# Attention block with adaLN and MLP: last query block in two halves, shift passes of 2048 columns into buffers of their own, zero matmuls inside PV, due points for side work

## The chip, the cores and the metric

The kernel runs on one core of a Trainium2 chip. The metric is the device time of one execution in microseconds; lower is better. Each kernel was run several times, and medians with the lowest and highest are quoted. Runs called slow (over 1.5% above the fastest of the same kernel) are left out of comparisons. The granted TensorE clock is quoted as a share of full speed. "Half clock" is the time at 0.50. In the trace of before a PV set (explained below) started 0.216 us after another at 1.00 and 0.426 us after another at 0.50 (medians of direct successors).

Engines: PE is TensorE, PEld its weight loads, DVE is VectorE, ACT is ScalarE, POOL is GpSimd, SP issues transfers.

## The reference

One sequence of 2048 tokens, 512 features, 32 heads of 16, an MLP of 1376. Modulation vectors come from a condition `c`.

```python
sa, ca, ga, sb, cb, gb = split(silu(c) @ w_mod, 6)
h = layernorm(x) * (1 + ca) + sa
q, k, v = heads(h @ wqkv)
o = softmax(q @ k.T * 16**-0.5) @ v
x = x + ga * (o @ wo)
h = layernorm(x) * (1 + cb) + sb
x = x + gb * (gelu(h @ w1 + b1) @ w2 + b2)
```

## The kernel before

Attention is cut into 32 runs: four blocks of 512 queries, and in each block eight runs of four heads. A run goes over 16 key tiles of 128 keys. A key tile gives two score pairs ("halves"), each 128x1024 in PSUM, the memory that TensorE writes its results to. PV is the product of the exponentials with V; the four matmuls that do it for one key tile are a PV set. ScalarE takes the exponential of most of them. For three key tiles of each run (none in run 0) VectorE takes over with integer arithmetic: one pass writes the bit pattern of a rough exponential, five "shift passes" write shifted copies, and six PV sets with six scaled copies of V add up to a good one. So a run has 26 exponentials on ScalarE and 31 PV sets on TensorE.

The program has no dynamic order. A small scheduler inside the kernel (a Plan) holds every operation with an assumed duration, walks through time, and emits instructions in the order that it finds; a wrong assumption is an order that fits the chip badly. A Plan operation takes a buffer (`acq`) and gives it back when the operations that name it in `rel` are done.

The score buffers and the buffers of the VectorE key tiles:

```python
r_st = res("st", 3, [P, 2 * QB], FP32, pp)       # score pairs, PSUM, for ScalarE and VectorE alike
r_pt = res("pt", NPT, [P, 2 * QB], BF16)         # exponentials of ScalarE, NPT = 9
r_ph = Res("ph", 2, lambda i: [work.tile([P, 2 * QB], I16, name=f"ph{i}_{j}")
                               for j in range(NPH)])          # a set of six for one half, two sets

def exp_d(qk, r, kt, half):                      # VectorE's key tile, one half
    def go(o):
        n_d[1] += 1
        nc.vector.tensor_scalar(out=o.tile[0], in0=qk.tile, scalar1=PH_B, scalar2=0.0,
                                op0=ALU.add, op1=ALU.max)
    e = op("DVE", go, 1.25, (qk,), lat=0.05, prio=0.5, acq=r_ph, rel=(qk,))
    sh = [e]
    for j in range(1, NPH):
        sh.append(op("DVE", lambda o, j=j: nc.vector.tensor_scalar(
            out=e.tile[j], in0=e.tile[0], scalar1=PH_SH[j], scalar2=None, op0=ALU.add),
            0.335, (e,), lat=0.1, prio=2.0))
    o_e[(r, kt, half)] = (e, sh)
    if half == 1:
        lo, shl = o_e.pop((r, kt, 0))
        # ... cut
        for j in range(NPH):
            pv_op(r, kt, j, (shl[j], sh[j]),
                  lambda j=j: [lo.tile[j].bitcast(BF16), e.tile[j].bitcast(BF16)], (lo, e))
```

The last argument of `pv_op` names what the PV set gives back. All six sets name both halves' sets of six buffers, so the buffers of a key tile come free after the last of its six PV sets, and with two sets only one key tile can be in work.

Keeping the TensorE clock up: the scheduler adds up the TensorE work of its last 3.4 us and, where it falls under `HEAT`, puts a matmul on zeros into a gap of TensorE, if the gap is long enough:

```python
for t, us in reversed(self.done):
    tot += us
    if tot >= HEAT and not self.cool:            # HEAT = 1.6 us
        self.cool = t + WIN                      # WIN = 3.4 us
```

The last query block: after the last run everything that follows attention (Wo, second norm, MLP) is done for all four token tiles of 128 at the end (`last_block`), while the same work of the other blocks (`block_tail`) is side work hidden in the attention of the next block.

The softmax here doesn't subtract the row's maximum and nothing guards it: scores larger than these inputs give would overflow.

## Time and profile before

Measured 962.17 us (median of 4 runs, 958.86 to 965.45). The profiled execution is not one of these four: it took 973 us, with a span of 971.3 us.

| stretch of the profiled execution | us |
|---|---|
| head, to the first exponential on ScalarE | 21.5 |
| run 0 | 48.6 |
| runs 1 to 31 | 857.9 |
| tail, after the last exponential | 43.3 |

The page of the kernel before: span, busy time of the engines, and the clock in 40 slices (tenths of full speed).

```profile
span 971.3 us, 18012 instructions
...
PE 845.8 (87%) x7140; PEld 287.1 (30%) x7140; DVE 739.6 (76%) x1499; ACT 834.7 (86%) x888; POOL 86.5 (9%) x189
...
PEclk9897999876579999999979999987999999999989
```

The windows view of the kernel before, for run 0, runs 1 to 31 in one stretch, and the tail. Columns: stretch, its length, busy time and number of instructions of PE, PEld, DVE, ACT and POOL, granted clock, share of DMA, GB/s.

```profile
21.50:70.10 48.60, 38.72 (x338) 19.44 (x338) 26.62 (x62) 35.84 (x42) 16.04 (x42) 0.93 0.10 33
70.10:928.00 857.90, 757.03 (x6521) 243.02 (x6521) 681.50 (x1368) 781.99 (x816) 59.98 (x67) 0.93 0.08 21
928.00:971.30 43.30, 31.48 (x186) 18.06 (x185) 21.73 (x42) 13.25 (x28) 3.19 (x8) 0.92 0.04 13
```

ScalarE is the spine: 838 exponentials start 0.904 us apart where nothing holds them up. In runs 1 to 31 it is busy 782 of 858 us; summing its idle times of that stretch gives 74.4 us, nearly all of it waiting for score matmuls. TensorE is not idle meanwhile. Taking from the trace what it executed just before the awaited scores, for the length of each of the 132 gaps, it was busy with PV of VectorE's key tiles (about 29 us), side work (about 26 us) and other PV (about 18 us) that stood before the awaited scores in its order. (No view gives these sums, and they move by some 3 us with how overlapping matmuls are counted.)

The chain of waits of the kernel before, from the tail: Wo of four tiles, transposes, and the last W2 tiles, one after the other.

```profile
928.47 3.13 PE st_13383 L787 x14
931.60 3.02 PE st_13384 L787 x14
...
941.58 0.94 PE st_13453 L905 x7
...
961.70 2.48 PE st_13653 L795 x11
...
964.49 2.50 PE ax_13671 L795 x11
```

### The profile page before, as it was taken

What the parts mean: (1) busy time and instruction counts of PE and PEld (TensorE: products, weight loads), DVE (VectorE), ACT (ScalarE), POOL (GpSimd) and SP (SyncE); (2) the same over time, 40 slices, a digit from 0 to 9 for tenths busy, and PEclk for the clock granted to TensorE, in tenths of its full rate; (3) what the DMA queues carried; (4) which work ended last, traced back from release to release, by engine and by line L of the source; (5) the groups of instructions that cost most, each with busy time, mean ns of one, the idle gap of its engine ahead of it and who ended that gap; (6) DMA issues with size and microseconds to landing.
All of it is one profiled execution on the core that took longest, in us unless ns stands there. A gap on an engine that the chain in (4) does not pass through costs nothing.

```text
span 971.3 us, 18012 instructions
## 1 busy us (share of the span) xinstructions
PE 845.8 (87%) x7140; PEld 287.1 (30%) x7140; DVE 739.6 (76%) x1499; ACT 834.7 (86%) x888; POOL 86.5 (9%) x189
## 2 busy tenths in 40 slices
PE   8788888889988988888998898889988889888868
PEld 3432333222222322222322232222332233222234
DVE  5738798766577988858877888857787989858862
ACT  2687998988689988998989989997999999999934
POOL 3331111000000100000000101000000001000010
PEclk9897999876579999999979999987999999999989
DMA  5105001001100000000100000000100000000100
GB/s 174 66 1 129 13 13 35 13 10 48 34 13 13 13 2 19 7 17 23 41 12 14 13 3 20 5 11 18 46 18 12 14 3 13 13 17 19 46 1 22
DMA packets 31038, 24.41 MB, mean 25 GB/s; under 512 B 13709, under 2 KB 26350, under 8 KB 30954
## 3 DMA queue, kind: packets, MB, share of 16 engines
q1 hardware_dynamic: 30426, 23.26, 8.4%
q8 instruction: 56, 0.92, 0.4%
q14 instruction: 28, 0.23, 0.1%
q10 hardware_dynamic: 528, 0.00, 0.0%
HBM read 20.64 MB, written 2.61 MB: 24 GB/s over the span
## 4 chain that ended last, share of the span: by engine, by line
PE 43%; ACT 38%; DVE 10%; issue 8%; POOL 0%; ACTq 0%; DVEq 0%; POOLq 0%
PE od_3149 L670 1%; PE od_3522 L670 1%; PE od_7084 L670 1%; PE od_2773 L670 1%; PE od_3903 L670 1%; PE od_5144 L670 1%; DVE ln_s L433 1%; PE od_1023 L670 1%; PE od_1461 L670 1%; PE od_9472 L670 1%; PE od_10639 L670 1%; PE od_7464 L670 1%; ACT g_11410 L831 1%; ACT g_8235 L831 1%; PE od_1921 L670 0%
## 5 line engine op out<-in xcount | busy, mean ns | idle before, releaser
L670 PEld LDWEIGHTS <-VEB_92 128*32 128x32 bf16 x512 | 13.6, 94 | 30.4 <-issue 29.1
L670 PEld LDWEIGHTS <-VEB_91 128*32 128x32 bf16 x512 | 14.9, 98 | 21.5 <-issue 18.3
L670 PEld LDWEIGHTS <-VEB_90 128*32 128x32 bf16 x512 | 13.2, 95 | 25.9 <-issue 24.1
L670 PEld LDWEIGHTS <-VEB_89 128*32 128x32 bf16 x512 | 12.5, 99 | 27.2 <-issue 25.5
L606 PEld LDWEIGHTS <-kT_2_114 32*128 32x128 bf16 x128 | 8.3, 91 | 26.3 <-issue 24.8
L824 PEld LDWEIGHTS <-W_83 128*128 128x128 bf16 x132 | 10.5, 99 | 16.6 <-issue 9.3
L606 PEld LDWEIGHTS <-kT_2_118 32*128 32x128 bf16 x128 | 7.4, 91 | 26.2 <-issue 25.7
L606 PEld LDWEIGHTS <-kT_2_122 32*128 32x128 bf16 x128 | 7.1, 93 | 26.3 <-issue 26.1
L606 PEld LDWEIGHTS <-kT_3_119 32*128 32x128 bf16 x128 | 7.8, 91 | 23.8 <-issue 23.3
L606 PEld LDWEIGHTS <-kT_2_110 32*128 32x128 bf16 x128 | 7.3, 91 | 25.3 <-issue 24.6
L606 PEld LDWEIGHTS <-kT_1_109 32*128 32x128 bf16 x128 | 6.9, 93 | 25.6 <-issue 23.0
L606 PEld LDWEIGHTS <-kT_3_111 32*128 32x128 bf16 x128 | 6.9, 91 | 24.5 <-issue 23.1
L606 PEld LDWEIGHTS <-kT_0_108 32*128 32x128 bf16 x128 | 7.2, 91 | 23.3 <-issue 21.9
L606 PEld LDWEIGHTS <-kT_1_117 32*128 32x128 bf16 x128 | 7.0, 92 | 23.2 <-issue 22.6
L606 PEld LDWEIGHTS <-kT_1_121 32*128 32x128 bf16 x128 | 6.6, 92 | 24.3 <-issue 24.1
L606 PEld LDWEIGHTS <-kT_0_120 32*128 32x128 bf16 x128 | 6.9, 93 | 22.7 <-issue 22.6
L449 ACT ACTIVATE blk_13381<-st_13453,modB 128x256 bf16<-128x256 bf16 x2 | 1.0, 560 | 14.5 <-PE st_13453 L905 14.5
L606 PEld LDWEIGHTS <-kT_0_112 32*128 32x128 bf16 x128 | 6.7, 91 | 22.6 <-issue 21.7
L606 PEld LDWEIGHTS <-kT_0_116 32*128 32x128 bf16 x128 | 6.9, 91 | 20.9 <-issue 19.8
L606 PEld LDWEIGHTS <-kT_3_123 32*128 32x128 bf16 x128 | 6.9, 93 | 20.9 <-issue 20.4
L606 PEld LDWEIGHTS <-kT_1_113 32*128 32x128 bf16 x128 | 6.9, 91 | 20.6 <-issue 20.1
L606 PEld LDWEIGHTS <-kT_3_115 32*128 32x128 bf16 x128 | 6.9, 91 | 20.0 <-issue 18.4
(5858 smaller groups left out, 3496.4 us busy)
## 6 DMA issues: line engine op xcount, KB each, us to landing
W_83<-in_B_w_dram SPq DMA_DIRECT2D x1, 1376.0 KB
g_998<-in_w_mod_dram SPq DMA_DIRECT2D x2, 512.0 KB
xb_127<-in_A_x_dram SPq DMA_DIRECT2D x1, 512.0 KB
blk_135<-in_w_mod_dram SPq DMA_DIRECT2D x1, 512.0 KB
blk_145<-in_w_mod_dram SPq DMA_DIRECT2D x1, 512.0 KB
w_171<-in_A_wqkv_dram SPq DMA_DIRECT2D x1, 512.0 KB
w_176<-in_A_wqkv_dram SPq DMA_DIRECT2D x1, 512.0 KB
xb_180<-in_A_x_dram SPq DMA_DIRECT2D x1, 512.0 KB
```

Of the source, the lines that this page charges most:

```text
L433: nc.vector.bn_stats(out=st6, in_=src)
L449: nc.scalar.activation(out=dst, in_=src, func=ACT.Identity, bias=mod[:, j:j + 1], scale=mod[:, NC + j:NC + j + 1])
L606: nc.tensor.matmul(out=o.tile[:, g * QB:(g + 1) * QB], lhsT=kT[cc][kb][rows, ko * P:(ko + 1) * P], rhs=qm.tile[par][rows, :], start=True, ...
L670: nc.tensor.matmul(out=o_od[r].tile[32 * i:32 * i + 32, :], lhsT=v_tile(kt, ph)[:, c0:c0 + 32], rhs=got[i // 2][:, (i % 2) * QB:(i % 2 + 1 ...
L824: nc.tensor.matmul(out=o.tile, lhsT=W1[:, j, f * P:(f + 1) * P], rhs=h.tile[:, j, :], start=(j == 0), stop=(j == NC - 1))
L831: ge = op("ACT", lambda o: nc.scalar.activation(out=g.tile, in_=g.tile, func=ACT.Gelu_apprx_tanh), 4.9 + 2.6, ev, lat=-1.2, prio=0.5)
```

## The change

The intent, as far as the diff shows it: take half of the tail into attention; keep the clock up with zero matmuls in the tile positions of PV; fewer and longer passes on VectorE; an earlier start; side work spread by due points (a due point is the number of exponentials done from which the scheduler prefers a piece of side work); and longer latencies assumed in the plan, meant to be nearer to the chip.

```diff
-HEAT = 1.6
+HEAT = 1.3
+PEL = 0.24   # assumed latency after a matmul, was 0.2 or 0.25
+DL = 0.14    # after a shift pass, was 0.1
+DPL = 0.08   # after VectorE's first pass, was 0.05
+AL = 0.17    # after an exponential, was 0.15

+        if o.kind == "pv" and s >= self.cool and o.last_left() > 1:
+            o.extra, o.us = True, 2 * o.us
...
+            if o.extra:
+                for i in range(4):
+                    nc.tensor.matmul(out=o_od[r].tile[32 * i:32 * i + 32, :], lhsT=warm[:, 0:32],
+                                     rhs=warm[:, 0:1].to_broadcast([P, QB]), start=False,
+                                     stop=False, tile_position=(0, 32 * i))

-    DKS = (2, 7, 12)
-    NPT = 9
+    DKS = (2, 6, 10, 14)        # three of these are used
+    NPT = 7
-    r_ph = Res("ph", 2, lambda i: [work.tile([P, 2 * QB], I16, name=f"ph{i}_{j}")
-                                   for j in range(NPH)])
+    r_ph = res("ph", 2, [P, 4 * QB], I16)
+    r_sh = res("sh", 4, [P, 4 * QB], I16)

     def exp_d(qk, r, kt, half):
+        first = o_e.pop((r, kt, 0)) if half else None
         def go(o):
             n_d[1] += 1
-            nc.vector.tensor_scalar(out=o.tile[0], in0=qk.tile, scalar1=PH_B, scalar2=0.0,
+            dst = (first or o).tile[:, half * 2 * QB:(half + 1) * 2 * QB]
+            nc.vector.tensor_scalar(out=dst, in0=qk.tile, scalar1=PH_B, scalar2=0.0,
                                     op0=ALU.add, op1=ALU.max)
-        e = op("DVE", go, 1.25, (qk,), lat=0.05, prio=0.5, acq=r_ph, rel=(qk,))
-        sh = [e]
+        e = op("DVE", go, 1.235, (qk, first), lat=DPL, prio=0.5, acq=None if half else r_ph,
+               rel=(qk,))
+        if not half:
+            o_e[(r, kt, 0)] = e
+            return
...
+        pv_op(r, kt, 0, (e,), parts(first), (first,))
         for j in range(1, NPH):
-            sh.append(op("DVE", lambda o, j=j: nc.vector.tensor_scalar(
-                out=e.tile[j], in0=e.tile[0], scalar1=PH_SH[j], scalar2=None, op0=ALU.add),
-                0.335, (e,), lat=0.1, prio=2.0))
...
+            sh = op("DVE", lambda o, j=j: nc.vector.tensor_scalar(
+                out=o.tile, in0=first.tile, scalar1=PH_SH[j], scalar2=None, op0=ALU.add),
+                0.595, (e,), lat=DL, prio=2.0, acq=r_sh, rel=(first,))
+            pv_op(r, kt, j, (sh,), parts(sh), (sh,))

-    o_x[0] = load_x(0)                                    # 512 tokens in one transfer
+    o_x0 = [dma(lambda o, t=t: nc.sync.dma_start(out=o_x[0].tile[:, t, :], in_=x_src[0][:, t, :]),
+                (o_x[0],), kb=128, prio=0.0) for t in range(TPB)]

+    def run_heads(r):            # last block: eight heads of 256 queries a run, else four of 512
+        b, u = runs[r]
+        return (u % NC, None, u // NC) if b == LAST else (u // 2, u % 2, None)

+        due(n_a[1] + 12, (TAIL if b < LAST - 1 else TAIL2 if b < LAST else TAIL3) / (9 * nt - 1))
...
-            if u == 7 and b < NQ - 1:
+            if u == 7 and b < LAST:
                 block_tail(b)
+            if u == NC - 1 and b == LAST:
+                block_tail(b, 2)                          # first half of the last block
             if r == NR - 1:
-                plan.heat = None
-                last_block(b)
+                last_half()
```

Cut: PV of the last block with eight matmuls of 256 columns in place of four of 512 (opened by zero matmuls with `start=True`); transposes of the input blocks in two steps; matmuls of zeros between the modulation columns; two x2 buffers in place of one and four q buffers in place of two; zero matmuls in the tail too; other assumed durations; smaller things.

## The prediction

> What bounds the kernel now. ScalarE's 838 exponentials (128x1024) are its spine. In the timeline they start 0.904 us apart (median), so the 26 of one run of attention need 23.5 us. Cut by exponentials: head 21.5 us; run 0 48.6 us (32 exponentials, ScalarE idle 14.2 us); runs 1 to 31 858 us, of which 18.6 us are three Gelu passes with table loads, so 27.1 us a run; tail after the last exponential 43.3 us. ScalarE's waits say that nearly all of its idle time in runs 1 to 31 (some 72 us) is for score matmuls.
>
> Much of that is the TensorE clock. The windows view gives clock 0.67 from 206.8 to 298.5 us, where runs take 28 to 32.7 us; at clock 1.00 (712 to 928 us) most take 24.8 to 26 us. The drops last multiples of 3.4 us, some 130 us in all before the tail. Counting the matmul columns of each 3.4 us window (score and PV matmuls at a quarter), drops follow windows with 0.9 to 1.3 us of full-array work. [...] this trace drops after thin ones. [...]
>
> What the change does, costed:
> - Zero matmuls inside PV (0.21 us, no change of tiling mode) are issued where the planned window is thin. I expect most of the half-clock time to go. The level planned for, 1.3, has no margin over what I read, so some drops stay.
> - Due points and truer latencies spread side work. Ten shift passes of 1024 columns per key tile, started 0.335 us apart, become five of 2048[...]. That saves about 0.37 us a key tile, 35 us of VectorE, which is not the bottleneck: a few us at most.
> - Together runs 1 to 31 go from 27.1 to about 25.8 us: minus 38 us.
> - Last block in halves: Wo, norm and MLP of two token tiles leave the tail. W1 on 256 tokens took 4.9 us, two W2 tiles 5.6 us, early Wo 16 x 0.215 us, the norm chain the rest. Tail 43.3 to about 29 us: minus 14. In exchange half a Gelu pass with two table loads goes between exponentials: plus 5 us. PV there takes eight matmuls of 256 columns for four of 512: TensorE time, estimated 1 us a run, mostly hidden.
> - First tokens by tile, transposes halved: head minus 1, run 0 minus 4 us, less certain.
> Sum: 963 - 38 - 14 + 5 - 5 = 911; I say 912.
>
> On the critical path: the tail fully; clock and score waits through ScalarE's idle time; shift passes hardly.
>
> What would show it: half clock outside the tail under 5%; ScalarE idle in runs 1 to 31 down from 72 to about 35 us; last exponential near 880 us, then 28 to 31 us; VectorE busy down by about 25 us.
>
> What would make it wrong: real windows thinner than planned, so drops remain; zero matmuls crowding TensorE, already busy 22 of 24 us in good runs; seven probability buffers in place of nine stalling ScalarE; split PV making the last eight runs TensorE-bound.

The 0.37 us a key tile follows from ten passes started 0.335 us apart, as in the trace of before, less five at the 0.595 us that the diff assumes; in the trace of after passes of 2048 columns start 0.602 us apart. The 1 us a run for the split PV was my estimate, and the trace of before has no such split to read it from.

## More of the kernel before

The plan has an end of its own: 923.4 us for this kernel.

The timeline of the kernel before, cut to one score pair that VectorE is to read (`st_13047`), and what VectorE does meanwhile. Columns: start, duration, engine, line, operation, written and read tiles, shapes.

```profile
905.61 0.39 PE L606 MATMUL st_13047<-qm_1_12217,kT_1_121 32*128 32x512 bf16 x2
...
906.07 0.42 DVE L641 TENSOR_SCALAR ph_1_12999<-ph_0_12998 128x1024 int16<-128x1024 int16 x1
...
907.41 0.42 DVE L641 TENSOR_SCALAR ph_5_13003<-ph_0_12998 128x1024 int16<-128x1024 int16 x1
...
907.75 0.42 DVE L641 TENSOR_SCALAR ph_1_13027<-ph_0_13026 128x1024 int16<-128x1024 int16 x1
...
909.20 0.41 DVE L641 TENSOR_SCALAR ph_5_13031<-ph_0_13026 128x1024 int16<-128x1024 int16 x1
...
909.52 1.21 DVE L636 TENSOR_SCALAR ph_0_13127<-st_13047 128x1024 int16<-128x1024 f32 x1
```

The pair is ready at 906.0 us and is read from 909.52 us on, after ten shift passes of the key tile before. For 3.5 us one of three score buffers is taken and idle.

## The result, and the profile after

902.75 us (median of 4 runs, 897.79 to 907.99), against 962.17: 59 us or 6.2% faster. The ratio of the fast runs is 0.938, 95% interval 0.932 to 0.945. Ratios here are the mean time of one kernel's fast runs over that of the other's of the same rounds, so not quite the ratio of the medians quoted.

| stretch of the profiled execution | before | after | difference | predicted |
|---|---|---|---|---|
| head | 21.5 | 17.1 | -4.4 | -1 |
| run 0 | 48.6 | 45.4 | -3.2 | -4 |
| runs 1 to 31 | 857.9 | 805.4 | -52.5 | -38 + 5 |
| tail | 43.3 | 31.4 | -11.9 | -14 |

The sum, -72, is more than the 59 of the medians, because the profiled execution of before is 11 us over its median and that of after 2 us under.

The page of the kernel after, the same three lines:

```profile
span 899.3 us, 20045 instructions
...
PE 810.7 (90%) x8359; PEld 301.1 (33%) x8359; DVE 709.7 (79%) x1047; ACT 822.4 (91%) x876; POOL 102.9 (11%) x231
...
PEclk9999999969799999999989999999999999999999
```

The windows view of the kernel after: run 0, runs 1 to 31, tail.

```profile
17.10:62.50 45.40, 38.79 (x373) 20.26 (x372) 28.81 (x70) 35.47 (x41) 22.53 (x63) 1.00 0.14 48
62.50:867.90 805.40, 733.76 (x7786) 264.35 (x7785) 653.62 (x927) 773.67 (x816) 69.98 (x80) 0.98 0.08 23
867.90:899.30 31.40, 23.47 (x124) 11.10 (x123) 15.81 (x26) 9.69 (x15) 1.94 (x4) 0.93 0.05 17
```

In runs 1 to 31 the clock rises from 0.93 to 0.98 (at half clock: 123 to 34 us), VectorE has 28 us less to do, and ScalarE's idle time falls from 74.4 to 28.9 us. All this fits the prediction, and any of the three might be the cause of the others. That is what the experiments are for.

The timeline of the kernel after, cut to two score pairs of one VectorE key tile (`st_12779`, `st_12829`, written into `ph_12807`) and the shift passes of the key tile before (`ph_12719`):

```profile
823.10 0.38 PE L653 MATMUL st_12779<-qm_9476,kT_1_122 32*128 32x512 bf16 x2
...
823.46 0.68 DVE L699 TENSOR_SCALAR sh_12792<-ph_12719 128x2048 int16<-128x2048 int16 x1
...
824.05 1.22 DVE L687 TENSOR_SCALAR ph_12807<-st_12779 128x1024 int16<-128x1024 f32 x1
...
825.54 0.39 PE L653 MATMUL st_12829<-qm_9476,kT_1_122 32*128 32x512 bf16 x2
...
826.39 1.21 DVE L687 TENSOR_SCALAR ph_12807<-st_12829 128x1024 int16<-128x1024 f32 x1
...
827.68 0.62 DVE L699 TENSOR_SCALAR sh_12879<-ph_12719 128x2048 int16<-128x2048 int16 x1
```

Each pair is read within 0.6 us of its end, in between shift passes of the tile before, which go on at 827.68. Two key tiles are in work.

The chain of waits of the kernel after, in the tail:

```profile
869.24 3.37 DVE OD_13721 L955 x2
...
878.68 3.17 PE ax_13774 L866 x8
...
883.50 0.40 PE ax_13806 L978 x4
```

The 3.17 us in the middle are W2 of the *first* half: its Gelu pass starts only when the last exponential is done (867.9 us), so half of the first half's MLP still stands in the tail.

### The profile page after: what moved, and what is told of

It is laid out like the page before. It is cut to its first block, busy times and chain, and to the rows that moved or that the text cites. A ratio compares the mean times of both kernels' runs of the same rounds, so it can differ in the third digit from the quotient of the medians.

```text
span 899.3 us, 20045 instructions
## 1 busy us (share of the span) xinstructions
PE 810.7 (90%) x8359; PEld 301.1 (33%) x8359; DVE 709.7 (79%) x1047; ACT 822.4 (91%) x876; POOL 102.9 (11%) x231
## 4 chain that ended last, share of the span: by engine, by line
ACT 44%; PE 32%; DVE 13%; issue 10%; POOL 1%; ACTq 0%; DVEq 0%; POOLq 0%
PE od_11734 L730 1%; PE od_3046 L730 1%; DVE ln_s L466 1%; PE od_4884 L730 1%; PE od_10747 L730 1%; ACT g_10663 L904 1%; ACT g_4545 L904 1%; ACT g_7500 L904 1%; PE od_3396 L730 1%; PE od_9655 L730 1%; PE od_6700 L730 0%; PE od_12755 L730 0%; PE od_3745 L730 0%; PE od_13256 L730 0%; ACT L673 0%
## 5 line engine op out<-in xcount | busy, mean ns | idle before, releaser
L730 PEld LDWEIGHTS <-VEB_89 128*32 128x32 bf16 x640 | 15.9, 97 | 25.5 <-issue 21.9
L730 PEld LDWEIGHTS <-VEB_92 128*32 128x32 bf16 x640 | 15.7, 95 | 22.8 <-issue 21.1
L730 PEld LDWEIGHTS <-VEB_91 128*32 128x32 bf16 x640 | 16.1, 96 | 16.8 <-issue 14.6
L730 PEld LDWEIGHTS <-VEB_90 128*32 128x32 bf16 x640 | 15.6, 96 | 15.7 <-issue 13.7
L897 PEld LDWEIGHTS <-W_83 128*128 128x128 bf16 x176 | 13.8, 97 | 18.1 <-issue 10.0
L653 PEld LDWEIGHTS <-kT_0_113 32*128 32x128 bf16 x128 | 6.8, 92 | 24.3 <-issue 21.9
L653 PEld LDWEIGHTS <-kT_0_125 32*128 32x128 bf16 x128 | 7.5, 91 | 21.4 <-issue 20.9
L653 PEld LDWEIGHTS <-kT_3_128 32*128 32x128 bf16 x128 | 7.0, 91 | 21.8 <-issue 21.3
L653 PEld LDWEIGHTS <-kT_2_127 32*128 32x128 bf16 x128 | 7.3, 91 | 20.4 <-issue 20.1
L653 PEld LDWEIGHTS <-kT_1_118 32*128 32x128 bf16 x128 | 6.8, 91 | 20.6 <-issue 19.9
L653 PEld LDWEIGHTS <-kT_3_124 32*128 32x128 bf16 x128 | 6.9, 91 | 19.6 <-issue 19.1
L653 PEld LDWEIGHTS <-kT_0_117 32*128 32x128 bf16 x128 | 6.7, 91 | 19.6 <-issue 18.4
L653 PEld LDWEIGHTS <-kT_0_121 32*128 32x128 bf16 x128 | 6.7, 91 | 19.4 <-issue 18.8
L653 PEld LDWEIGHTS <-kT_1_114 32*128 32x128 bf16 x128 | 6.6, 91 | 19.8 <-issue 18.0
L653 PEld LDWEIGHTS <-kT_1_122 32*128 32x128 bf16 x128 | 6.9, 91 | 18.5 <-issue 17.9
L653 PEld LDWEIGHTS <-kT_2_119 32*128 32x128 bf16 x128 | 6.9, 91 | 17.6 <-issue 16.9
L653 PEld LDWEIGHTS <-kT_2_123 32*128 32x128 bf16 x128 | 6.5, 91 | 18.9 <-issue 18.7
L653 PEld LDWEIGHTS <-kT_1_126 32*128 32x128 bf16 x128 | 6.9, 92 | 17.5 <-issue 17.0
L653 PEld LDWEIGHTS <-kT_3_116 32*128 32x128 bf16 x128 | 6.1, 90 | 19.0 <-issue 17.6
L653 PEld LDWEIGHTS <-kT_2_115 32*128 32x128 bf16 x128 | 6.5, 91 | 17.2 <-issue 16.1
L653 PEld LDWEIGHTS <-kT_3_120 32*128 32x128 bf16 x128 | 6.4, 91 | 17.2 <-issue 16.7
```

The lines of the kernel that those rows point to most:

```text
L653: nc.tensor.matmul(out=o.tile[:, g * QB:(g + 1) * QB], lhsT=kT[cc][kb][rows, ko * P:(ko + 1) * P], rhs=qm.tile[rows, par, :] if hb is None ...
L730: nc.tensor.matmul(out=o_od[r].tile[32 * i:32 * i + 32, n * HB:n * HB + w], lhsT=v_tile(kt, ph)[:, c0:c0 + 32], rhs=got[i // 2][:, at:at + ...
L897: nc.tensor.matmul(out=o.tile[:, 0:N], lhsT=W1[:, j, f * P:(f + 1) * P], rhs=h.tile[:, j, 0:N], start=(j == 0), stop=(j == NC - 1))
```

## The experiments

Twelve kernels were run. Each was timed in three rounds beside the kernel before. The numbers of a profiled execution are in the table at the end of this section. "Plan's own end" in the expectations is the end that the kernel's scheduler computes for its own order; it is no measurement, and it is quoted only to say how far a new order differs.

A word on noise. Each kernel has four runs, and their ratio to before is known to some 0.6%, or 6 us. The intervals of four kernels that differ from the change by 7 to 11 us (zero matmuls not issued, constant moved, last block whole, more zeros) overlap a little with that of the change, 0.932 to 0.945. These differences are likely but rough. Those of the two kernels that exchange the shift code, 39 and 53 us, are far outside the noise.

First four: one thing changed in the changed kernel (the first two keep its plan), and the yardstick.

### Zero matmuls inside PV planned but not issued

```diff
-            if o.extra:
+            if o.extra and False:
```

> The changed kernel with the same plan and the same order on every engine; only the 212 zero matmuls inside PV are planned but not issued. Theory (the clock is about half of the gain of runs 1 to 31): half-clock time before the tail rises from 34 us to over 90 us and the time from 903 to 915 to 930 us. Rival (planning alone made the runs shorter): within 4 us of 903, whatever the clock does.

Measured 913.91 us (911.31 to 919.36), ratio to before 0.950 against 0.938. Half-clock time in runs 1 to 31 rose from 34 to 89 us, ScalarE's idle time from 29 to 43. So the zero matmuls (53 sets of four) are worth 11 us here, at 0.2 us for each us at half clock. Both numbers lie just under the expected range (915 us, over 90 us at half clock), outside that of the rival, and the clock is a fifth of the gain, not half.

### Shift passes issued as two of 1024 columns

```diff
-            sh = op("DVE", lambda o, j=j: nc.vector.tensor_scalar(
-                out=o.tile, in0=first.tile, scalar1=PH_SH[j], scalar2=None, op0=ALU.add),
+            sh = op("DVE", lambda o, j=j: [nc.vector.tensor_scalar(
+                out=o.tile[:, c:c + 2 * QB], in0=first.tile[:, c:c + 2 * QB], scalar1=PH_SH[j],
+                scalar2=None, op0=ALU.add) for c in (0, 2 * QB)],
```

> The changed kernel with the same plan and order; each of the 465 shift passes of 2048 columns is issued as two of 1024. VectorE busy time rises by about 35 us (710 to 745). Theory (VectorE is not the bottleneck): under 6 us slower than 903. Rival (wide passes relieve the waits for scores): 15 us slower or more.

Two of the four runs were slow, among them the profiled one, and are left out. The two fast runs took 907.7 and 898.84 us; their ratio to before is 0.938, the same as that of the change. VectorE's busy time rose to 733 us in the profiled execution, by 24 us and not by 35. In this order of instructions the width of a pass costs nothing that can be seen in two runs. (The interval, 0.930 to 0.947, allows some 8 us.)

### First tokens in one transfer

```diff
-    o_x0 = [dma(... one token tile of 128 KB ...) for t in range(TPB)]
+    o_x[0] = load_x(0)
+    o_x0 = [o_x[0]] * TPB
```

> The changed kernel with the first 512 tokens loaded by one transfer of 512 KB in place of four of 128 KB. Theory (most of the 4.4 us won in the head are the earlier first tile): the first exponential comes at 20 to 21.5 us in place of 17.1, and the time is 3 to 4 us longer. Rival (the head won by the halved transposes and the order of q and k): first exponential within 1.5 us of 17.1.

902.37 us (901.18 to 907.81): no difference. The first exponential came at 19.3 us in place of 17.1, between the two expectations, but run 0 took 40.8 us in place of 45.4, and the last exponential ended at 867.9 us in both kernels.

The windows view of this kernel, head and run 0 left out: runs 1 to 31.

```profile
60.10:867.90 807.80, 734.41 (x7787) 264.19 (x7787) 658.43 (x930) 773.27 (x816) 77.16 (x85) 0.97 0.08 22
```

What the head wins is given back in run 0, presumably because run 0 waits for keys and values of the later blocks anyway; no run shows this by itself. I had counted it as won.

### A planning constant moved by 5 ns

```diff
-AL = 0.17
+AL = 0.165
```

> The changed kernel with one planning constant moved by 5 ns (the assumed latency after an exponential 0.165 in place of 0.17 us), which has no meaning of its own but makes another plan. It measures what a new plan alone does: expected within 5 us of 903 either way. Effects of later experiments that make a new plan count only above this.

911.25 us (906.5 to 912.55): 8.5 us slower, more than expected, with 68 us at half clock in place of 34. A meaningless change to a static plan moved the time by 8.5 us. This is one sample, and it holds the noise of the runs as well. Every experiment that makes a new plan is judged against this; those that keep the plan (the first two, and two of the next four) are not touched by it. It also says that some of the 59 us may be the luck of a chosen plan.

Next four: parts alone, and parts undone.

### The kernel before with zero matmuls inside PV, plan untouched

```diff
+        if o.kind == "pv" and s >= self.cool2 and o.last_left() > 1:     # window under 1.3 us
+            o.extra = True
... and the same zero matmuls in PV as in the change
```

> The kernel before, its plan and order untouched; 142 sets of four zero matmuls are added inside PV where its own plan has less than 1.3 us of TensorE work in 3.4 us. The mirror image of taking them out of the changed kernel, which cost 11 us. Theory (half-clock time costs about 0.25 us per us): clock from 0.945 to about 0.965, time from 963 to 950 to 956. Rival (zero matmuls crowd a TensorE that has no room): 963 or slower.

964.9 us (957.62 to 968.46), ratio to before 1.0025, interval 0.996 to 1.009: no gain, although the clock of its runs was 0.965 to 0.979, where listed runs of the kernel before have 0.935 to 0.957. The 0.25 us per us in the expectation was my estimate; the profiled executions of the first experiment and of the change give 0.26 (915.32 - 901.08 = 14 us for 55 us), their medians 0.2.

The windows view of this kernel, runs 1 to 31:

```profile
70.50:922.30 851.80, 737.97 (x6998) 248.65 (x7085) 681.40 (x1368) 781.08 (x816) 61.41 (x67) 0.97 0.08 21
```

Half-clock time fell to 48 us, but ScalarE still idled 68.7 us. The rival won, with no gain; its reason, that zero matmuls crowd TensorE, was not shown. That does not yet acquit the clock. This is no mirror image: 142 sets were added here, 53 are in the change, and what 142 sets cost may hide what the clock won. The traces can part the two. Of the 74.4 us that ScalarE idled in the kernel before, only 26.0 ended in the 123 us at half clock; 48.4 ended at full clock. So most of the waiting was not the clock's doing; see the end of this section.

### The last block attended whole, in the changed kernel

```diff
-        return (u % NC, None, u // NC) if b == LAST else (u // 2, u % 2, None)
+        return u // 2, u % 2, None
... and last_block in place of block_tail(b, 2) and last_half
```

> The changed kernel with the last query block attended whole and with the tail of the kernel before. Theory: the time after the last exponential goes from 31.4 back to about 43 us and the whole is 10 to 18 us longer than 903, more than the 8.5 us by which a mere new plan moved it. Rival (halving the block costs inside attention what it saves behind it): within 8 us of 903 although the tail is 12 us longer, because the last exponential comes earlier.

912.63 us (906.81 to 915.82), 10 us slower, at the lower edge of what was expected and hardly more than a new plan alone. But the parts can be read one by one: the tail is 43.0 us in place of 31.4, and the last eight runs 208.1 in place of 210.8. Halving saves 11.6 us behind attention and costs 2.7 us in it (the second is small against what a new plan does).

### The kernel before with the latencies of the change

```diff
-lat=0.2 / 0.25 after matmuls, 0.15 after exponentials, 0.05 and 0.1 on VectorE
+lat=0.24, 0.17, 0.08 and 0.14
```

> The kernel before with only the planning constants for latencies moved to those of the change (0.24 after a matmul, 0.17 after an exponential, 0.08 and 0.14 on VectorE, 0.071 per small projection matmul). Theory (truer latencies carry most of the shorter runs at full clock): 940 to 952. Rival (due points, buffers and the halved block carry them): 955 to 968, within what a new plan alone does.

962.12 us (955.36 to 969.14), ratio 1.0006: nothing. The longer latencies alone do not carry the gain.

### 64 more sets of zero matmuls, plan untouched

```diff
+        elif o.kind == "pv" and s >= self.cool2 and o.last_left() > 1:   # window under 1.4 us
+            o.extra = True
```

> The changed kernel, plan and order untouched, with 64 more sets of zero matmuls where the planned window has under 1.4 us of work. If the remaining half-clock time (34 us before the tail) still costs 0.25 us per us, the time falls from 903 to 894 to 900 and the clock rises from 0.976 to over 0.985. Rival (TensorE too full): 903 or more.

910.06 us (904.58 to 914.53), 7 us slower, the clock unchanged (0.963 to 0.978). That is what the rival expected: these zero matmuls, which the plan does not know of, saved nothing and probably cost time. In the changed kernel the planned ones are already enough.

At this point the clock was worth 11 us, the tail 9, head and latencies nothing, and some 39 us had no owner. What was left of the change was the code of the VectorE key tiles. Hence the last four.

### The changed kernel with the old code of the shift passes

```diff
-    r_ph = res("ph", 2, [P, 4 * QB], I16)
-    r_sh = res("sh", 4, [P, 4 * QB], I16)
+    r_ph = Res("ph", 2, lambda i: [work.tile([P, 2 * QB], I16, name=f"ph{i}_{j}")
+                                   for j in range(NPH)])
... and exp_d as before, with the assumed durations of the change
```

> The changed kernel with the code of the shift passes as before: ten passes of 1024 columns a key tile, half 0's passes independent of half 1, one set of six buffers per half that comes free only after its last PV. Everything else as changed, newly planned (the plan's own end moves from 891.5 to 930). Theory (the new arrangement of the VectorE key tiles, not the width of a pass, carries most of the shorter runs, because score buffers are no longer held up): 925 to 945 us, score buffers held by VectorE back from 336 to over 450 us in sum, ScalarE idle in runs 1 to 31 from 29 to over 50 us. Rival (due points, zeros and the halved block carry them): within 8.5 us of 903, as any new plan.

956.24 us (951.13 to 958.36), ratio to before 0.991. Undoing this one part takes back 53 of the 59 us, with everything else of the change in place. That is more than expected (925 to 945 us). VectorE held its score buffers for 482 us in sum (from the end of the score matmuls to the end of the pass that reads them), where over 450 was expected and the change has 336.

The page and the windows view (runs 1 to 31) of this kernel:

```profile
span 953.3 us, 20904 instructions
...
PE 834.7 (88%) x8560; PEld 309.1 (32%) x8560; DVE 749.8 (79%) x1512; ACT 831.8 (87%) x878; POOL 97.2 (10%) x231
```

```profile
62.80:919.60 856.80, 755.30 (x7987) 271.79 (x7986) 693.85 (x1392) 786.17 (x819) 64.16 (x80) 0.96 0.08 21
```

The 856.8 us of runs 1 to 31 are those of the kernel before (857.9), at a clock of 0.96 in place of 0.93. But they are spread otherwise. Runs 1 to 23 take 625 us (before 642, changed 595), and the last eight, with the halved block, 231 us (before 216, changed 211). So some 21 of the 53 us are lost in the halved block alone, which goes badly with the old code: the 53 us hold an interaction and are not the worth of the new code by itself.

### The kernel before with the new code of the shift passes

```diff
+    r_ph = res("ph", 2, [P, 4 * QB], I16)
+    r_sh = res("sh", 4, [P, 4 * QB], I16)
... and exp_d as changed, with the latencies of before; waits on x2 added
```

> The kernel before with only the shift passes of the change (both halves in one tile, five passes of 2048 columns each into a buffer of its own, planned at 0.595 us). Waits on the x2 buffer are added where the new plan needs them; alone they leave the plan of before as it was. The plan's own end moves from 923.4 to 900.7. Theory: 935 to 950 us (from 962), with the sum of score holding under 400 us. Rival: within 8.5 us of 962.

924.32 us (922.23 to 932.0), ratio to before 0.960: 39 us faster by this part alone, more than expected. VectorE held its score buffers for 329 us (under 400 expected; 505 in the kernel before).

The page and the windows view (runs 1 to 31) of this kernel:

```profile
span 922.5 us, 17564 instructions
...
PE 821.4 (89%) x7124; PEld 281.0 (30%) x7124; DVE 698.5 (76%) x1034; ACT 828.0 (90%) x888; POOL 87.7 (10%) x189
```

```profile
68.80:875.90 807.10, 733.00 (x6498) 236.82 (x6498) 639.09 (x901) 775.34 (x816) 61.22 (x67) 0.96 0.08 21
```

Runs 1 to 31 take 807.1 us, as in the changed kernel (805.4), with none of its zero matmuls in PV, due points or latencies.

### The same with narrow passes

```diff
-                0.595, (e,), lat=0.1, prio=2.0, acq=r_sh, rel=(first,))     # one pass of 2048
+                0.67, (e,), lat=0.1, prio=2.0, acq=r_sh, rel=(first,))      # issued as two of 1024
```

> As the kernel before with the new shift passes, but each pass of 2048 columns is issued, and planned at 0.67 us, as two of 1024, so that VectorE has as much to do as before. Theory (order and buffers matter, not width): within 8.5 us of the variant with wide passes. Rival (width matters): back within 8.5 us of 962.

931.71 us (929.61 to 947.71; the 947.71 is a slow run and left out of the ratio, 0.965). VectorE has 26 us of its work in runs 1 to 31 back (665 us; 639 with wide passes, 681.5 in the kernel before), and 31 of the 39 us stay. The 7 us between the two lie within what a new plan does. So the width is not what matters, within these 8 us.

### A new plan

```diff
-TAIL, CB = 150, 40; TAIL2, TAIL3 = 120, 90; APR = 26; FILL = 1.6; HEAT = 1.3
+TAIL, CB = 200, 52; TAIL2, TAIL3 = 160, 95; APR = 25.5; FILL = 1.7; HEAT = 1.4
-                     acq=(r_st, r_ax)[half])     # second transpose of the tail
+                     acq=r_st)
```

> An attempt to beat both: the changed kernel with other planning constants (tails spread over 200, 160 and 95 exponentials in place of 150, 120 and 90; window level 1.4 in place of 1.3; fill 1.7; other due points) and the second transpose of the tail in a score buffer. Its plan ends at 884.3 in place of 891.5. Measured times have been 11 to 17 us over the plan, so 893 to 903; if a plan's luck on the chip decides, anything from 895 to 911.

898.37 us (896.79 to 899.15), ratio to before 0.931, interval 0.925 to 0.937, against 0.938 (0.932 to 0.945) of the change. It beats the kernel before; that it beats the change is likely but not shown, since the intervals overlap. The tail is 29.4 us in place of 31.4.

### All of them side by side

From the profiled executions; runs 1 to 31 only, except for the last column. "Wait of VectorE's scores" is the sum, over the 186 score pairs that VectorE reads, of the time from the end of the score matmuls to the start of the pass that reads them. (Which pairs these are follows from the order in which the kernel emits its score matmuls; no view of the profile gives the sum.) The kernel with two slow runs is left out.

| kernel | shift code | us | at half clock | wait of VectorE's scores | ScalarE idle | median of all |
|---|---|---|---|---|---|---|
| before | old | 857.9 | 123 | 278 | 74.4 | 962.2 |
| before + zero matmuls | old | 851.9 | 48 | 281 | 68.7 | 964.9 |
| before + latencies | old | 839.0 | 65 | 255 | 55.2 | 962.1 |
| changed, old shift code | old | 856.8 | 61 | 255 | 68.5 | 956.2 |
| before, new shift code | new | 807.1 | 68 | 102 | 30.2 | 924.3 |
| the same, narrow passes | new | 811.6 | 75 | 135 | 31.6 | 931.7 |
| changed | new | 805.3 | 34 | 110 | 28.9 | 902.8 |
| changed, PV zeros not issued | new | 818.9 | 89 | 106 | 43.0 | 913.9 |
| changed, one first transfer | new | 807.7 | 41 | 115 | 32.6 | 902.4 |
| changed, constant moved | new | 817.3 | 68 | 121 | 40.7 | 911.3 |
| changed, last block whole | new | 799.5 | 21 | 96 | 26.0 | 912.6 |
| changed, more zeros | new | 809.6 | 38 | 110 | 34.0 | 910.1 |
| new plan | new | 807.8 | 48 | 90 | 29.9 | 898.4 |

Read by columns: the half-clock time overlaps between the two groups, and the idle time does not follow it from one group to the other. "Changed, old shift code" and "before, new shift code" are at half clock equally long (61 and 68 us) and idle 68.5 and 30.2 us. The wait of VectorE's scores splits the kernels into two groups without overlap, 255 to 281 and 90 to 135 us, and so does the idle time of ScalarE, 55 to 74 and 26 to 43 us. Inside the new group the half-clock time does matter: from 21 to 89 us the idle time goes from 26 to 43.

The sharpest test of the clock leaves out all time at half clock. Counting only gaps of ScalarE that ended at full clock, it idled 48.4 of 735 us in the kernel before and 58.1 of 796 us in "changed, old shift code", against 18.4 of 739 us in "before, new shift code" and 24.6 of 771 us in the changed kernel. (Gaps of over 0.15 us of the traces, as in the column; no view gives the split.) At the same clock the old code idles two to three times as much.

## Why the prediction was right or wrong

The number was right: 912 us predicted, 902.75 measured. The reason given for most of it was not, so that the number fits is in good part luck: the clock brought less than was counted on, and the new shift code, counted at a few us, brought 39.

**"Much of that is the TensorE clock."** This step failed. The clock did what was predicted (half clock fell from 123 to 34 us in runs 1 to 31, 3.9% of the time before the tail, where under 5% was forecast), but most of ScalarE's idle time was not its work: 48.4 of 74.4 us fell at full clock. In the changed kernel 55 us more at half clock cost 11 us. In the kernel before, cutting the half-clock time from 123 to 48 us with zero matmuls left the time where it was (1.0025), though there the cost of the zero matmuls may have hidden a gain of that size. I had seen slow runs with a low clock and taken the one for the cause of all; at a clock of 1.00 the runs of the kernel before were late as well, 24.8 to 26 us and more against a floor of 23.5, and that rest I called planning without asking what in the plan.

**"VectorE ... is not the bottleneck: a few us at most."** Half of this was right and the wrong half decided. VectorE's time did fall by about the forecast amount (740 to 710 us; shift passes of 2048 columns start 0.602 us apart in the trace, where the diff assumes 0.595), and it is worth little: narrow passes in the same order cost nothing that could be seen (two fast runs). But I costed the width and passed over the buffers. The code of the shift passes is worth 39 us alone and 53 us when it is taken out of the change. These two numbers overlap with the other parts' and are not to be added to them.

How it works, as far as it is shown: three score buffers in PSUM serve ScalarE and VectorE. In the old code VectorE's next key tile is read only after the shift passes of the one before, since in the plan its two sets of buffers come free after the last PV set; the timeline shows a pair waiting 3.5 us. While VectorE's pair waits, ScalarE has two buffers left, scores can't be computed ahead, and PV and side work stand before them in TensorE's order. With the new code the wait of these pairs falls by 60%, and ScalarE's idle time with it, in every kernel that has it and in none that has not. That the wait is the link between the code and the idle time is the explanation that fits all of these runs; no run changed the wait by itself. Nor is it settled which of the three new things in the code does it: own buffers for the shifted copies, both halves in one tile (so that the second pair is read before any shift pass), or two key tiles in work. Only the width is excluded, within some 8 us.

**Runs 1 to 31, minus 38 and plus 5.** -52.5 in the profiled executions. The plus 5 for half a Gelu pass between exponentials did not come: the pass runs after the last exponential, where ScalarE has nothing else to do. Of the other 14 us, 11 can be the profiled execution of before, which was that much over its median.

**Tail, 43.3 to about 29.** 31.4. The mechanism was right. The 2 us too much are probably W2 of the first half, which the chain of waits shows in the middle of the tail (3.17 us); in the new plan, with the second transpose in another buffer, the tail is 29.4 us. The split costs 2.7 us in the last eight runs, where I had said 1 us a run, mostly hidden.

**Head minus 1, run 0 minus 4.** -4.4 and -3.2 in the profiles, but the earlier first tile is worth nothing: without it the head is 2.2 us longer and run 0 is 4.6 us shorter.

**What would make it wrong.** Zero matmuls may have crowded TensorE where the plan did not know of them: with 64 more sets the median is 7 us longer. Seven probability buffers in place of nine did not stall ScalarE so that it could be seen; that was not tried by itself.

Left open: the moved key tiles of VectorE (2, 6, 10 in place of 2, 7, 12) were not tried by themselves, and due points could not be tested alone. Without them the scheduler did not find a complete order (side work of one block still held buffers that the next needed), so no such kernel exists to run. The new shift code (39 us), the tail (9 us net) and the planned zero matmuls (11 us), set side by side, come to the 59 us measured. Such effects need not add, so this is a hint and no proof that due points and latencies give less than the 8.5 us of a new plan.

## What to carry to other kernels

When a queue of few buffers feeds two consumers, look at how long each consumer leaves a full buffer unread: the slower consumer may starve the faster one although it is not the bottleneck itself (here the explanation that fits, not one shown by itself). When a diff makes an operation wider, cost separately what it does to the owners and the release of buffers, and to the order; here the width was worth nothing that could be seen, and the release and order 39 us. And in a kernel with a static plan, run a change without meaning first: here 5 ns in one constant moved the median by 8.5 us, which is the yardstick for every other experiment.

## What the traces show of the clock

- In the traces of before and after half clock comes in stretches of one to six times 3.41 us (not counting the last, which the end of the program cuts off). It followed thin windows. Counting full-array work in windows of 3.41 us (32-row and 32-column matmuls of 512 columns at a quarter, which is my way of counting; how narrow tiles count was not shown): in the kernel before, of windows at full clock with under 1.1 us of work 8 of 8 were followed by half clock, of those with 1.1 to 1.4 us 8 of 23, of those with more 0 of 207. After: 4 of 5, 3 of 24, 0 of 219. At half clock, windows with at least 1.3 us (which then take 2.6 us, three quarters of the window) were followed by full clock in 12 of 14 cases before, thinner ones in 4 of 26. The counts are made from the clock records and matmuls of the traces; no view gives them. A recount with other rules for matmuls that straddle two windows moves them by one to three; one that counts a full-array matmul of 512 columns, and a PV set, at the set's measured 0.216 us puts a dozen windows of before over the bound of 1.4 us (10 of 11, 6 of 10, 1 of 218). The picture stays.
- Time at half clock cost the changed kernel 0.2 us for each us (11 us for 55, zero matmuls inside PV not issued), and in the kernel before nothing that could be seen, once zero matmuls had to be issued to avoid it (ratio 1.0025).
- One execution of this one-core kernel had a granted clock of 0.841 in the mean: 0.88 in its first 100 us, then 0.84, 0.84 and 0.85 in the stretches looked at (300 to 400, 600 to 700 and 800 to 868 us). What else ran on the die is not known. The cores view of that execution (the kernel with shift passes issued as two of 1024):

```profile
core: us from the first to the last instruction, mean granted TensorE clock
core 0: 918.9 us, clock 0.841
```
